# Block-sparse attention and a top-2 expert layer on one core: where keys are scaled, who turns rows, and which banks the products share

## The chip, the cores and the metric

The kernel runs on one core of a Trainium2 chip. The metric is the device time of one execution in microseconds (us). A core has engines with a queue of instructions each: TensorE (PE, matrix products, with its weight loads shown apart as PEld), VectorE (DVE), ScalarE (ACT), GpSimd (POOL) and SyncE (SP), which here only starts DMA transfers. Instructions of one queue run in the order of the code, and semaphores hold an instruction back until what it needs is done. Products land in PSUM, which has eight banks of 128 partitions and 512 numbers of 32 bits.

## The reference, cut to what matters

```python
# q, k, v: 4 batches, 8 heads, 768 positions, 64 numbers a head; blocks of 32 positions
mask = np.abs(blk_i - blk_j) <= 1
mask = mask | (blk_i == 0) | (blk_j == 0) | (blk_i == n_blocks - 1) | (blk_j == n_blocks - 1)
for qb in range(n_blocks):
    for kb in sampled_blocks[qb]:          # 3 sampled blocks for each query block
        mask[qb * block:(qb + 1) * block, kb * block:(kb + 1) * block] = True
scores = np.where(mask, scale * np.matmul(q, k.transpose(0, 1, 3, 2)), -1e9)   # scale = 1/8
attn = exp(scores - max) / sum
x = np.matmul(attn, v) as rows             # 3072 rows of 512 numbers

noisy = x @ w_gate + log1p(exp(x @ w_noise)) * noise      # 8 experts
top2, weights = the two largest of noisy, softmax over the two
out[row] += weight * (relu(x[row] @ w1[e]) @ w2[e])       # for the two experts e of each row
```

## The kernel before, in words

The order of the code is the order on each engine's queue (a manual schedule). Attention comes first, the routing to experts runs between its steps, and the experts follow.

A batch has six tiles of 128 queries (`t`), each in two halves of four heads (`f`); the queries of the first and last block, which see every key, are four further items (`g`, the global rows). `steps` walks over the 64 items of all batches. At step k four items are in work at different stages: `new` (item k+2) gets its scores and its softmax, `now` (item k) has its exponentials turned by PE (`turn`, tile `ptr`), `old` (item k-1) gets its products with v (`av`, into the PSUM tile `po`) and is divided by its sums (`norm`, tile `xr`), and `out` (item k-2) is split into two 16-bit halves by ACT (`high`, L382) and POOL (`low`, L389). Two steps later PE turns the finished rows (`turn_x`, L396) for the routing and the result is copied out to `r_xT` (L397).

PSUM: six banks `ps` for scores and turned exponentials, one bank `po` which `av`, `turn_x` and the routing's products share, and one bank `pog`, in which the global rows' products (`global_av`, L352) gather over a batch.

Keys: `kk` holds a whole batch, loaded by SP in six pieces (`load_k`, L169) while the batch before is in work. For each tile, POOL copies the key blocks that it needs into `kc` (`prefetch_k`, L200 and L201; two buffers), and `scores` (L238) multiplies queries by `kc`, or by `kk` for the global rows (`qg`). The factor 1/8 is put on the queries by POOL (`scale`, L180), once for each tile and each `qg`.

Values: SP loads, for each tile and half of its blocks, the windows of neighbours (L212) and then, block by block, the sampled blocks (L216, each one small transfer whose address is read from a register). POOL writes the columns of weights (`weigh`, L224). `va` and `vb` have three buffers up to the fourth batch and two in it.

Routing: `Router.run` is a generator whose pieces are done at `background`; its products go to `po` as well (L678, L754), and DVE keeps sums in `r_acc` (L756). Its constants, `r_d` (POOL, L543) and `r_tri` (DVE, L545) among them, are made in the first batch. `store` (L586) writes the rows to `x_rows`. Near the end of attention POOL gathers the rows of the experts' first unit (L945), and SP turns them by DMA into `xta` (`xpose`, L955), which the first products of the experts (L1003) read. Weights for them come in pieces and are cut to 16 bits by ACT (`w1s`, L889).

## Time and profile before

| what | us |
|---|---|
| three timed executions | 861.63, 868.29, 869.1 (median 868.29) |
| the profiled execution | 863.63 |
| its span, first to last instruction | 861.8 |
| PE busy in it | 789.2 (92%) |
| DVE, ACT, POOL busy | 568.7, 366.9, 388.1 |

The profiled execution's own time is 1.8 us above its span. The busy times are of the whole span; attention takes the first 318.6 us of it and the experts the rest. Matmuls overlap their weight loads, and the granted clock of PE (PEclk in the rows below) is a share of full speed.

### The profile page before, as it was taken

The numbers are of one execution on the slowest core, as the hardware profiler recorded it, in microseconds if no ns is written. First come the engines' busy times: TensorE is split into PE (matmuls) and PEld (weight loads), VectorE is DVE, ScalarE is ACT, GpSimd is POOL, SyncE is SP. The second block draws the span as 40 slices with busy tenths as digits, with TensorE's granted clock in tenths as the row PEclk, the third lists the DMA queues.
The fourth block names the chain that finished last, engine by engine and source line by source line (L and its number), as shares of the span: only waits on it lengthen the run. The fifth ranks groups of instructions, "written<-read, shape, count | busy, mean of one in ns | idle before, by whom it ended". The sixth has DMA issues, their size and how long they took to land.

```text
span 861.8 us, 25602 instructions
## 1 busy us (share of the span) xinstructions
PE 789.2 (92%) x9823; PEld 484.6 (56%) x9823; DVE 568.7 (66%) x1197; ACT 366.9 (43%) x698; POOL 388.1 (45%) x672
## 2 busy tenths in 40 slices
PE   7878988988876779999999989999999999999995
PEld 4556666666654557566587544554554554554552
DVE  6566888878796537762133378697697796796621
ACT  4747757656653415321022331542642633543500
POOL 5566577667558330132245426426335345323211
PEclk9989999999998889999999999999999999999998
DMA  4686677776688985856169939639538548533301
GB/s 150 179 235 201 185 213 192 209 213 187 193 283 260 250 207 151 196 181 112 49 155 224 242 111 233 191 99 237 173 111 238 164 123 221 164 98 102 100 33 49
DMA packets 119848, 148.92 MB, mean 173 GB/s; under 512 B 69515, under 2 KB 76300, under 8 KB 119714
## 3 DMA queue, kind: packets, MB, share of 16 engines
q1 hardware_dynamic: 107490, 109.22, 48.6%
q0 software_dynamic: 12224, 37.96, 13.6%
q8 instruction: 79, 1.29, 0.6%
q14 instruction: 55, 0.45, 0.2%
HBM read 107.28 MB, written 26.15 MB: 155 GB/s over the span
## 4 chain that ended last, share of the span: by engine, by line
PE 75%; DVE 12%; issue 5%; ACT 3%; POOL 2%; DMA 1%; SPq 0%; POOLq 0%; DVEq 0%; ACTq 0%
PE pc L1089 29%; PE pa L1042 10%; PE ps L238 6%; PE pa L1003 6%; PE pd L1042 5%; PE po L326 4%; PE pd L1003 4%; PE ps L304 3%; DVE m L277 3%; PE pc L1098 3%; PE pc L1042 2%; PE po L396 1%; PE pog L352 1%; DMA va<-in_vx_dram 1%; DVE xr L336 1%
## 5 line engine op out<-in xcount | busy, mean ns | idle before, releaser
L1089 PE MATMUL pc<-w,hh 128*128 128x512 f16 x768 | 228.4, 379 | 0.0
L1122 POOL DMA_INDIRECT out_dram<-y,r_xT x46 | 66.9, 1454 | 210.2 <-DVE y L1121 176.7
L1089 PE MATMUL pc<-w,hl 128*128 128x512 f16 x384 | 145.5, 379 | 0.0
L1089 PEld LDWEIGHTS <-hh 128*128 128x128 f16 x768 | 74.6, 98 | 86.3
L1042 PEld LDWEIGHTS <-w 128*128 128x128 f16 x840 | 82.2, 98 | 63.1
L280 ACT ACTIVATE p<-ps,m 128x256 f32<-128x256 f32 x192 | 75.2, 475 | 62.8 <-DVE m L277 61.2
L1011 ACT ACTIVATE hh<-pa 128x408 f16<-128x408 f32 (+2 forms) x60 | 26.3, 447 | 121.9 <-PE pa L1003 116.4
L200 POOL COPY kc<-kk 128x128 f32 x264 | 69.2, 300 | 14.0 <-PE ps L238 9.1
L277 DVE TENSOR_REDUCE m<-ps 128x2 f32<-128x512 f32 x96 | 61.6, 682 | 17.2 <-PE ps L238 16.9
L893 DVE SCALAR_TENSOR_TENSOR w<-wraw,w 128x1024 f16<-128x1024 f32 (+1 forms) x58 | 65.2, 1127 | 10.6 <-ACT w L889 10.6
L326 PE MATMUL po<-va,ptr 128*32 128x68 f32 x1536 | 57.4, 235 | 14.8 <-DMA va<-in_vx_dram 4.5
L238 PE MATMUL ps<-kc,q 64*32 64x256 f32 x1536 | 58.8, 399 | 7.5 <-POOL q L180 4.5
L1014 DVE SCALAR_TENSOR_TENSOR hl<-pa,hh 128x408 f16<-128x408 f32 (+2 forms) x60 | 30.1, 503 | 51.9 <-ACT hh L1011 51.9
L945 POOL DMA_INDIRECT xg<-x_rows,r_xT x46 | 57.3, 1246 | 14.7 <-issue 14.1
L963 POOL DMA_INDIRECT pv<-out_dram,r_xT x44 | 48.7, 1107 | 32.0 <-issue 29.0
L1089 PEld LDWEIGHTS <-hl 128*128 128x128 f16 x384 | 37.6, 98 | 45.3
L326 PEld LDWEIGHTS po<-va,ptr 128*32 128x32 f32 x1536 | 40.8, 115 | 36.6 <-issue 13.2
L326 PE MATMUL po<-vb,ptr 128*32 128x68 f32 x1536 | 56.6, 232 | 5.2 <-issue 5.2
L889 ACT ACTIVATE w<-wraw 128x1024 f16<-128x1024 f32 (+1 forms) x58 | 56.4, 975 | 6.6 <-DMA wraw<-in_moe_w_dram 6.6
L1121 DVE SCALAR_TENSOR_TENSOR y<-pc,r_xT,pv 128x512 f32<-128x512 f32 x37 | 27.7, 750 | 47.4 <-PE pc L1089 47.4
L304 PE MATMUL ps<-r_ident,p 128*128 128x128 f32 x384 | 54.0, 284 | 0.7 <-issue 0.6
L1003 PEld LDWEIGHTS <-w1s 128*128 128x128 f16 x432 | 43.0, 100 | 13.9 <-issue 0.9
(231 smaller groups left out, 1576.7 us busy)
## 6 DMA issues: line engine op xcount, KB each, us to landing
wraw<-in_moe_w_dram SPq DMA_DIRECT2D x64, 512.0 KB, 4.5
va<-in_vw_dram SPq DMA_DIRECT2D x40, 384.0 KB, 4.8
vb<-in_vx_dram SPq DMA_DIRECT2D x176, 64.0 KB, 3.4
q<-in_qt_dram SPq DMA_DIRECT2D x24, 256.0 KB, 3.3
va<-in_vx_dram SPq DMA_DIRECT2D x88, 64.0 KB, 4.1
kk<-in_kt_dram SPq DMA_DIRECT2D x18, 256.0 KB, 2.9
x_rows<-x SPq DMA_DIRECT2D x16, 256.0 KB, 3.2
out_dram<-x SPq DMA_DIRECT2D x4, 768.0 KB
```

What stands on the lines that cost most here:

```text
L200: nc.gpsimd.tensor_copy(kc[:, j, :, 3 + n], flat[:, bass.ds(self.listed(blk, n), P)].rearrange("p (n c) -> p n c", c=32))
L238: mm = lambda o, l, r: nc.tensor.matmul(o, l, r, start=True, stop=True, skip_group_check=True)
L277: nc.vector.tensor_reduce(m[:, par], s[par].rearrange("p (e c) -> p e c", e=2), axis=AX.X, op=ALU.max, negate=True)
L280: nc.scalar.activation(p[:, 2 * e + par], s[par][:, 256 * e:256 * e + 256], AF.Exp, bias=m[:, par, e:e + 1])
L304: nc.tensor.transpose(t[:, e, c], p[:, 2 * e + par, P * c:P * c + P], self.ident)
L326: nc.tensor.matmul(o[32 * j:32 * j + 32, h], d[:, h % 2, h // 2, x, 32 * j:32 * j + 32], self.values(v[:, self.slot(t, j)], 4 * f + h), st ...
L893: self.nc.vector.scalar_tensor_tensor(lo, t, WS, hi, op0=ALU.mult, op1=ALU.subtract)
L945: nc.gpsimd.indirect_dma_start(out=self.xg[0:m, c + self.place(u)], out_offset=None, in_=self.x_dram[0:nr], in_offset=bass.IndirectOffsetO ...
L1003: nc.tensor.matmul(ph[:, 0:m], w[:, wt, slot, kb % 2 * P:kb % 2 * P + P], r["xt"][:, kb, a, o:o + m], start=i == 0, stop=i == last)
L1042: nc.tensor.matmul(o, w[:, wt, slot, s * P:s * P + P], mv(s, a), start=i == 0 and p in tail, stop=i == 5, skip_group_check=True)
L1089: nc.tensor.matmul(py, h[:, f, o], w(f)[:, x], start=i == 0, stop=i == last)
L1122: d = nc.gpsimd.indirect_dma_start(out=self.out, out_offset=bass.IndirectOffsetOnAxis(ap=r["ix"][0:m, c:c + 1], axis=0), in_=y[0:m], in_of ...
```

## The change

Four things are changed in attention and one call in the experts.

1. `ps_o` gets two banks, used by turns, and `pog` is dropped. `global_av` now puts the products of one tile into a `po` bank, and DVE copies (first tile of a batch) or adds them to the SBUF tile `og`. It is called ahead of the `av` of the same item instead of behind its `norm`.
2. `turn_x` is copied out by ACT instead of DVE.
3. Keys are scaled instead of queries: at the start the two halves of `kk` by DVE and POOL, later each of the six pieces of the next batch by POOL, two steps after its load is issued. The `scale` of `q` and `qg` is gone.
4. The query pool has three buffers instead of four, and queries are loaded at most two tiles ahead.
5. `xpose` of unit 0 (five DMA transposes) is issued by ACT's queue instead of SP's.

```diff
--- before.py
+++ after.py
@@ -72,14 +72,13 @@
         pool = lambda c, name, bufs, **kw: c.enter_context(tc.tile_pool(name=name, bufs=bufs, **kw))
         self.const = pool(ctx, "aconst", 1, side="right")
         self.buf = pool(ctx, "abuf", 1, side="right")
-        self.qp = pool(ctx, "aq", 4, side="right")
+        self.qp = pool(ctx, "aq", 3, side="right")
         self.pp = pool(ctx, "app", 2, side="right")
         self.gp = pool(early, "agp", 3)
         self.sm = pool(ctx, "asm", 4, side="right")
         self.xp = pool(ctx, "axp", 2, side="right")
         self.ps_s = pool(ctx, "ps_s", 6, space=PSUM)
-        self.ps_o = pool(ctx, "ps_o", 1, space=PSUM)
-        self.ps_g = pool(ctx, "ps_g", 1, space=PSUM)
+        self.ps_o = pool(ctx, "ps_o", 2, space=PSUM)
         ep = pool(early, "aeb", 1)
         two = lambda n: ep if n == 2 else self.buf
         J = self.NJ
@@ -90,6 +89,7 @@
         self.qgt = [two(2 - 2 * i).tile([P, self.NP, 64], F32, name=f"qg{i}") for i in range(2)]
         self.ends = [two(2).tile([P, self.HD], F32, name=f"ends{i}") for i in range(2)]
         self.xs = [self.buf.tile([P, self.NP, 2, P], F16, name=f"x{n}") for n in range(2)]
+        self.og = self.const.tile([P, 4, self.W], F32, name="og")
         self.known = self.const.tile([P, self.NB, 2], F32, name="known")
         self.pgt = [self.buf.tile([P, 8, P], F32, name=f"pgt{i}") for i in range(4)]
         self.ident = ident
@@ -176,8 +176,9 @@
     def load_ends(self, b):
         self.nc.sync.dma_start(self.ends[b % 2][64:128], self.vg[b])
 
-    def scale(self, x):
-        self.nc.gpsimd.tensor_scalar(x, x, 0.125, 1.0, op0=ALU.mult, op1=ALU.mult)
+    def scale_k(self, b, i, n, engine):
+        x = self.kk[b % 2][:, i * self.NB // n:(i + 1) * self.NB // n]
+        engine.tensor_scalar(x, x, 0.125, 1.0, op0=ALU.mult, op1=ALU.mult)
 
     def which(self, b, t):
         n = b * self.T + t
@@ -339,19 +340,20 @@
     def global_av(self, b, t):
         nc, W = self.nc, self.W
         va = self.st["v", b, t][0]
-        if t == 0:
-            self.og = self.ps_g.tile([P, 512], F32, name="pog")[:, 0:4 * W].rearrange("p (i r w) -> p i r w", i=2, r=2)
-        for c in range(8):
-            blk = 3 * c + 1
-            if blk // self.NJ != t:
-                continue
+        cs = [c for c in range(8) if (3 * c + 1) // self.NJ == t]
+        o = self.psum()[:, 0:4 * W].rearrange("p (i w) -> p i w", w=W)
+        for c in cs:
             for i in range(2):
                 for r in range(2):
                     for e in range(2):
                         h = 2 * (2 * i + e) + r
-                        nc.tensor.matmul(self.og[64 * e:64 * e + 64, i, r], self.pgt[2 * i + r][0:96, c, 64 * e:64 * e + 64],
-                                         self.values(va[0:96, blk % self.NJ], h), start=c == 0 and i == 0 and r == 0,
-                                         stop=c == 7, skip_group_check=True)
+                        nc.tensor.matmul(o[64 * e:64 * e + 64, 2 * i + r], self.pgt[2 * i + r][0:96, c, 64 * e:64 * e + 64],
+                                         self.values(va[0:96, (3 * c + 1) % self.NJ], h),
+                                         start=c == cs[0] and i == 0 and r == 0, stop=c == cs[-1], skip_group_check=True)
+        if t == 0:
+            nc.vector.tensor_copy(self.og, o)
+        else:
+            nc.vector.tensor_tensor(self.og, self.og, o, op=ALU.add)
 
     def x_tile(self, b, t):
         if ("x", b, t) not in self.st:
@@ -363,7 +365,7 @@
     def global_out(self, b, part):
         nc = self.nc
         if part == 0:
-            self.xgr = self.norm(self.og.rearrange("p i r w -> p (i r) w"), 4)
+            self.xgr = self.norm(self.og, 4)
             self.xg = self.xp.tile([P, 2, 2, P], F16, name="xg", bufs=1)
         elif part == 1:
             nc.scalar.activation(self.xg[:, :, 0], self.xgr.rearrange("p (i r) d -> p i (r d)", i=2), AF.Copy)
@@ -394,7 +396,7 @@
         o = self.psum().bitcast(F16).rearrange("p (c k) -> p c k", c=2 * self.NP)
         for c in range(2 * self.NP):
             nc.tensor.transpose(o[:, c], x[:, c], self.ident16)
-        nc.vector.tensor_copy(xT[:, t].rearrange("p k a c -> p (k a) c"), o)
+        nc.scalar.activation(xT[:, t].rearrange("p k a c -> p (k a) c"), o, AF.Copy)
 
     def warm(self):
         o = self.bank()
@@ -409,13 +411,13 @@
             self.load_k(0, i, 2)
         self.prefetch_q(0, 0)
         self.listed = self.numbers(self.packed, mybir.EngineType.Pool, P)
-        self.scale(self.st["qg", 0])
+        for i, engine in enumerate((self.nc.vector, self.nc.gpsimd)):
+            self.scale_k(0, i, 2, engine)
         for x in self.va:
             self.nc.vector.memset(x[0:96, :, self.HD:], 1.0 / XS)
         for x in self.vb:
             self.nc.vector.memset(x[64:P, :, self.HD:], 1.0 / XS)
         self.prefetch_k(0, 0)
-        self.scale(self.st["q", 0, 0])
         self.load_ends(0)
         self.unlisted = self.numbers(self.masked, mybir.EngineType.SP, 1)
         self.prefetch_v(0, 0, 0)
@@ -427,14 +429,13 @@
         self.prefetch_v(0, 1, 0)
         self.prefetch_v(0, 1, 1)
         self.weigh(0, 1)
-        self.scale(self.st["q", 0, 1])
 
     def steps(self, router, done, background):
         nc, T, B = self.nc, self.T, self.B
         n = len(self.items)
         get = lambda k: self.items[k] if 0 <= k < n else ("none",)
         tg = [(b, t) for b in range(B) for t in range(T)]
-        nq, nz, nk, nv = 3, 2, 2, 2
+        nq, nk, nv = 3, 2, 2
         turns, shares, stores, halves = [], [], [], []
         marks = [(n - 1, self.spread, n // 2, (n % 2 * 2,)) for n in range(4)]
         for k in range(-2, n + 7):
@@ -459,10 +460,10 @@
             self.cut(now)
             background(k, 1)
             if old[0] == "q":
+                if old[3] == 1:
+                    self.global_av(old[1], old[2])
                 self.av(old)
                 self.st[old, "xr"] = self.norm(self.st.pop((old, "o")), 4)
-                if old[3] == 1:
-                    self.global_av(old[1], old[2])
             background(k, 2)
             while shares:
                 b, part = shares.pop(0)
@@ -475,20 +476,17 @@
             if old[0] == "q" and old[3] == 1 and old[2] == T - 1:
                 self.global_out(old[1], 0)
                 shares.append((old[1], 1))
-            if nz < nq and new[0] == "q" and new[3] == 0 and new != ("q", 0, 0, 0):
-                self.scale(self.st[("q",) + tg[nz]])
-                nz += 1
             if new[0] == "q" and new[1] + 1 < B:
                 i = 2 * new[2] + new[3] - 1
                 if i == 2:
                     self.load_g(new[1] + 1)
                     self.load_ends(new[1] + 1)
-                if i == 7:
-                    self.scale(self.st["qg", new[1] + 1])
+                if 2 <= i <= 7:
+                    self.scale_k(new[1] + 1, i - 2, 6, nc.gpsimd)
             if new[0] == "q" and new[3] == 1 and nk < len(tg):
                 self.prefetch_k(*tg[nk])
                 nk += 1
-            if new[0] == "q" and nq < len(tg) and (nq > self.late_) == (new[3] == 1):
+            if new[0] == "q" and nq < min(len(tg), new[1] * T + new[2] + 3) and (nq > self.late_) == (new[3] == 1):
                 self.prefetch_q(*tg[nq])
                 nq += 1
             while halves:
@@ -952,7 +950,7 @@
         if c == 0:
             pool, x = (self.xta, "a") if u % 2 == 0 else (self.xtb, "b")
             r["xt"] = pool.tile([P, self.KB, 2, 7 * P], F16, name="xt" + x)
-        self.nc.sync.dma_start_transpose(out=r["xt"][:, :, :, c * P:(c + 1) * P].rearrange("p k a r -> p (k a) r"),
+        (self.nc.scalar if u == 0 else self.nc.sync).dma_start_transpose(out=r["xt"][:, :, :, c * P:(c + 1) * P].rearrange("p k a r -> p (k a) r"),
                                          in_=self.xg[:, c + self.place(u)])
 
     def gather_prev(self, u):
```

On POOL's queue, in the first batch before the copies of tile 3 (`xe` is the 16-bit form of rows of the tiles that hold global rows, `kk_105` the current batch's keys), there stood before:

```order
L201 COPY kc_107<-kk_105 128x4x96
L389 TENSOR_TENSOR xe<-xr,xe 128x2x128
L180 TENSOR_SCALAR q<-q 128x512
L200 REGISTER_ALU
L200 ISA
L200 COPY kc_108<-kk_105 128x4x32
```

and now (`kk_102` is the current batch's keys, `kk_103` the next batch's):

```order
L202 COPY kc_104<-kk_102 128x4x96
L391 TENSOR_TENSOR xe<-xr,xe 128x2x128
L181 TENSOR_SCALAR kk_103<-kk_103 128x512
L201 REGISTER_ALU
L201 ISA
L201 COPY kc_105<-kk_102 128x4x32
```

The scale there is no longer one of a query tile but one of a piece of the next batch's keys.

Some 40 rows later on the same queue, where the routing's constants are made, there stood before:

```order
L389 TENSOR_TENSOR xe<-xr,xe 128x2x128
L180 TENSOR_SCALAR q<-q 128x512
L224 COPY va_99<-known 128x4x32
L224 COPY vb_102<-known 128x4x32
L543 IOTA r_d 128x128
L549 IOTA r_io_825 128x8
L552 IOTA r_tok 128x6
L554 IOTA r_line 128x128
```

and now:

```order
L391 TENSOR_TENSOR xe<-xr,xe 128x2x128
L181 TENSOR_SCALAR kk_103<-kk_103 128x512
L225 COPY va_96<-known 128x4x32
L225 COPY vb_99<-known 128x4x32
L541 IOTA r_d 128x128
L547 IOTA r_io_821 128x8
L550 IOTA r_tok 128x6
L552 IOTA r_line 128x128
L181 TENSOR_SCALAR kk_103<-kk_103 128x512
```

A second piece of keys stands ahead of the constants in place of a query tile, and a third behind them.

On ACT's queue, at the last weights (`w1s`) before the end of attention, there stood before:

```order
L280 ACTIVATE p<-ps,m 128x256 x4
L889 ACTIVATE w1s<-wraw 128x1024
L306 ACTIVATE ptr<-ps 128x512
L382 ACTIVATE x_113<-xr 128x2x128
L280 ACTIVATE p<-ps,m 128x256 x4
L306 ACTIVATE ptr<-ps 128x512
```

and now:

```order
L281 ACTIVATE p<-ps,m 128x256 x4
L887 ACTIVATE w1s<-wraw 128x1024
L953 DMA_TRANSPOSE xta<-xg 128x8x128 x2
L307 ACTIVATE ptr<-ps 128x512
L384 ACTIVATE x_110<-xr 128x2x128
L399 ACTIVATE r_xT<-po 128x1024
L281 ACTIVATE p<-ps,m 128x256 x4
L953 DMA_TRANSPOSE xta<-xg 128x8x128 x2
L307 ACTIVATE ptr<-ps 128x512
```

The four transposes stand between ACT's own steps, and so does the eviction of the turned x, `r_xT`; a fifth transpose follows two rows later.

## Rows read from the trace of the kernel before

**Rows 1.** Windows: length, busy us per engine (instructions), PEclk, DMA share, GB/s.

```profile
0.00:80.00 80.00, 62.98 (x1381) 43.34 (x1382) 49.94 (x130) 47.80 (x105) 48.59 (x159) 0.96 0.66 188
80.00:235.00 155.00, 134.84 (x3389) 96.64 (x3387) 126.77 (x354) 101.90 (x227) 100.25 (x259) 1.00 0.71 199
235.00:318.60 83.60, 59.72 (x1428) 44.45 (x1428) 55.49 (x162) 32.37 (x79) 47.63 (x102) 0.91 0.90 247
318.60:862.00 543.40, 531.61 (x3628) 300.16 (x3627) 336.50 (x554) 184.80 (x289) 191.59 (x154) 0.99 0.56 151
```

**Rows 2.** PE's waits, 80 to 235 us: total, times, longest.

```profile
PE po L396 <- DVE xr L336: 4.1, 4, 1.4
PE po L678 <- DVE xr L336: 2.4, 2, 1.2
PE po L326 <- DVE r_acc L756: 2.1, 2, 1.5
```

**Rows 3.** Groups by shape, DVE, 0 to 318 us: busy, mean ns.

```profile
L336 DVE TENSOR_TENSOR xr<-po,rc 128x256 f32<-128x256 f32 x48 | 20.4, 425 | 4.0
...
L397 DVE COPY r_xT<-po 128x1024 f16<-128x1024 f16 x24 | 16.4, 683 | 1.7 <-PE po L396 0.9
```

**Rows 4.** Groups by shape, ACT, 0 to 318 us.

```profile
L306 ACT ACTIVATE ptr<-ps 128x512 f32<-128x512 f32 x48 | 28.9, 603 | 27.8 <-PE ps L304 27.5
```

**Rows 5.** Groups by shape, POOL, 0 to 318 us.

```profile
L180 POOL TENSOR_SCALAR q<-q 128x512 f32<-128x512 f32 x24 | 14.8, 619 | 12.1 <-DMA q<-in_qt_dram 12.1
```

**Rows 6.** Line L216 on SP's queue, 80 to 235 us: min/median/max ns.

```profile
L216 SPq DMA_DIRECT2D vb<-in_vx_dram x99: 315/316/1127, 81.3 to 234.9; - x99
```

**Rows 7.** SP's timeline, 133.5 to 140 us: start, duration.

```profile
137.57 0.97 SPq L216 DMA_DIRECT2D vb<-in_vx_dram  x2
```

**Rows 8.** Line L326 on PE, 141 to 143.3 us: first and last start.

```profile
L326 PE MATMUL po<-va,ptr x32: 222/223/247, 142.0 to 142.8; 128*32 128x68 f32 x32
```

**Rows 9.** POOL's timeline, 28 to 56 us: idle before in brackets.

```profile
33.03 0.77 POOL L200 COPY kc<-kk 128x128 f32 x3
...
37.69 0.68 POOL L389 TENSOR_TENSOR xe<-xr,xe 128x256 f16<-128x256 f32 x1
44.69 0.62 POOL L180 TENSOR_SCALAR q<-q 128x512 f32<-128x512 f32 x1 [6.33 <-DMA q<-in_qt_dram]
...
45.73 0.24 POOL L543 IOTA r_d<- 128x128 int32 x1
```

**Rows 10.** DVE's timeline, 37 to 48 us.

```profile
46.01 0.23 DVE L545 TENSOR_SCALAR r_tri<-r_d 128x128 f16<-128x128 int32 x1 [7.96 <-POOL r_d L543]
```

**Rows 11.** PE's timeline, 40 to 57 us.

```profile
47.65 1.96 PE L238 MATMUL ps<-kc,q 64*32 64x256 f32 x30 [1.22 <-DVE ptr L308]
```

**Rows 12.** SP's timeline, 40 to 52 us.

```profile
40.76 1.51 SPq L191 DMA_DIRECT2D q<-in_qt_dram  x1
```

**Rows 13.** Tile kk, 100 to 140 us: issues and landing.

```profile
L169 SPq DMA_DIRECT2D kk<-in_kt_dram x6: 416/526/1302, 109.0 to 132.8; - x6
...
DMA to landing us min/median/max: 2.8/2.8/2.8
```

**Rows 14.** POOL's timeline, 103 to 128 us.

```profile
104.98 0.77 POOL L200 COPY kc<-kk 128x128 f32 x3 [1.57 <-PE ps L238]
```

**Rows 15.** Line L238 on PE, 113 to 127 us: first and last start.

```profile
L238 PE MATMUL ps<-kc,q x96: 372/376/401, 114.6 to 126.2; 64*32 64x256 f32 x96
```

**Rows 16.** Chain of waits, 240 to 320 us: start, us, what.

```profile
291.08 6.83 DMA va<-in_vx_dram
```

**Rows 17.** SP's timeline, 280 to 306 us.

```profile
294.77 0.34 SPq L212 DMA_DIRECT2D va<-in_vw_dram  x1
...
299.69 3.29 SPq L955 DMA_TRANSPOSE xta<-xg  x2
```

**Rows 18.** ACT's timeline, 284 to 319 us.

```profile
289.29 1.07 ACT L889 ACTIVATE w1s<-wraw 128x1024 f16<-128x1024 f32 x1
```

**Rows 19.** Windows, 298 to 302 us.

```profile
298.00:302.00 4.00, 4.00 (x66) 3.56 (x66) 1.43 (x4) 0.00 (x0) 0.00 (x0) 0.50 1.02 167
```

## Prediction, made before the changed kernel ran

> **What bounds the kernel now.** I read the windows first: in the experts' stage, from 318.6 us to the end, TensorE (PE) is busy for 531.6 of 543.4 us, and the diff touches nothing there but who issues five transposes ahead of it. Whatever the change does, it does in the 318.6 us of attention. There PE is idle for 17 us in the first 80, 20 in the next 155 and 24 in the last 84; the reader should see that VectorE (DVE), with 126.8 of 155 us in the middle stretch, is nearly as full as PE [rows 1]. So nothing in the middle stretch can be worth more than some 20 us. Next I read what PE waits for there: the largest items that name the single `po` bank are the turned x behind `xr` (4.1 us), the routing's sums behind `xr` (2.4) and av behind the routing's `r_acc` (2.1) [rows 2].
>
> Then I looked for what stands behind PE, and found SyncE's (SP's) queue. It carries every load of v; L216 alone issues 149 small DMAs in that stretch, 99 of them for `vb`, each 0.32 us at the median [rows 6], with a starting distance of about 0.65 us, since two issued together take 0.97 us of timeline [rows 7]. For tile 10 the last pair of these is issued up to 138.54 (137.57 + 0.97) [rows 7], and PE starts its product with v at 142.0 [rows 8]. With a landing of 2.8 us, which I read from the keys [rows 13], the data are there at 141.3: PE can be 0.7 us earlier in that place, no more, unless SP is too. So I take SP as the pacemaker of the later tiles of each batch; only the first tiles of a batch, beside the global rows, give it a lead.
>
> **Two banks, and the eviction by ScalarE (ACT).** Of PE's waits the three items above make 8.6 us in 155 [rows 2]; the same rate over the 83.6 us after it makes 4.6 more. Not every such wait ends with a second bank, so I take 12 us of these 13.2. DVE loses 24 copies of 0.683 us (16.4 us) and gains 24 adds or copies of 128x272 numbers, which I price as `xr`, 128x256 from the same kind of bank, 0.425 us (10.2 us) [rows 3]: 6.2 us less. ACT gains 24 evictions of 1024 columns. Its 512 columns take 0.603 us [rows 4], so one takes between 0.6 and 1.2; I take 1.0, 24 us in all. ACT is busy 101.9 of 155 us there [rows 1], so this fits beside other work, but the turned x stays in its bank 0.3 us longer than before. Gain if PE alone set the pace: 12 us. Gain that SP's queue lets through: 0.7 us as at tile 10, once in each of four batches and not added up, because SP's issues don't move: about 1 us.
>
> **Keys scaled in place of queries.** GpSimd (POOL) loses 24 scales of 0.619 us [rows 5] and four smaller ones; it gains one half of 128x1536 at the start and 18 scales of 128x512 at the same 0.619. In busy time that is nothing. The start costs at most 3 x 0.619 = 1.9 us on POOL against what it did before, and at 44.69 POOL has 6.33 us of idle time to spend [rows 9], so I charge 0. What matters is the wait. A scale of a piece of the *next* batch's keys waits for that piece's DMA, and behind it on POOL stand the copies `kc` for the current batch, which PE's scores need.
>
> Batch 0: before, the copies of tile 3 run from 33.03 to 37.69, 4.7 us, and only then does POOL wait, for a query load, to 44.69; `r_d` is made at 45.73 [rows 9], DVE's `r_tri` has waited 7.96 us for that [rows 10], and PE's scores start again at 47.65 [rows 11]. After, the first key piece stands ahead of tile 3's copies and takes the place on SP that the query load had, issued at 40.76 [rows 12]. It lands when that one did, at 44.6. Then 0.6 scale, 4.7 copies, 0.7 `xe`, 0.6 next scale, 0.5 the two `known` copies: `r_d` at 51.8, 6.1 us later than 45.73. PE's waits of that place are already behind this chain, so all 6.1 us is on the path.
>
> Batch 1: pieces are issued from 109.0 and land 2.8 us later [rows 13]; with an issue of 1.0 us, the first is there at 112.2 or later (an `x_rows` issue beside it moves this by no more than 0.5). The copies behind it began at 104.98 [rows 14] and now begin at 112.8, 7.8 us later. Before, they ended at 109.7 (4.7 us later) and their scores began at 114.6 [rows 15], 4.9 us of slack: 7.8 - 4.9 = 2.9 us. The scores go through the copies one after the other, so part of this is hidden; I take 2. For the next tile and for the same places of batch 2 I have no row as near and take 2.5 and 0.8, as estimates from this one; batch 3 has no keys to scale. Sum 6.1 + 2 + 2.5 + 0.8 = 11.4 us of delay. Bounds: 0, if the pieces come earlier because SP's queue does, and 11.4.
>
> How much of it is left at the end? SP's issues are not delayed by it as long as the buffers of v are free, and PE, with 12 us fewer waits for the bank, catches up with SP: by the first term it can regain up to 12 us where it is behind. So delay and gain nearly cancel: 11.4 - 12 gives -0.6 where SP sets no pace, and where it does the time can't fall below before's by more than 1. I take +0.5 for the first 235 us.
>
> **Unit 0's transposes on ACT.** SP is relieved of 3.29 us between the two halves of v of the last tile [rows 17]. That is on PE's path only in part: the long wait of this stretch comes earlier, for a `va` that stands in the chain as one transfer of 6.83 us from 291.08 [rows 16]. In the order of after, the first two transposes stand on ACT right behind `w1s`, which ends at 290.36 (289.29 + 1.07) [rows 18], 9.3 us earlier than on SP. The DMA engines are full there: share 0.90 over the whole last stretch [rows 1] and 1.02 in 298 to 302, where PE also runs at a granted clock of 0.50, that is 1.2 GHz, after its wait [rows 19]. So two transposes' transfers get in front of v for tiles 22 and 23. I price that between 0 and 3.3 us, the time the pair takes to issue; nearest is the middle, since other transfers are in flight beside it: +1.7. On the other side SP's next issues come 3.3 us earlier: up to -3.3, of which half reaches PE, -1.6, as the bank and norm chain ends late too. ACT, which issues them, is held for 3.3 us behind `w1s`, at a time when PE waits for `va` anyway; 0. Later q loads for the last tiles put 512 KB into the full stretch: +0.5.
>
> The Trainium skill, "Trainium Kernel Development and Optimization", section Key Constraints, says that DMAs from the SP, ACT and POOL queues all run on the same 16 engines and interleave, and that issuing from several only saves the issuing sequencer's time. By that rule the move is worth at most SP's issue time and the full DMA share agrees with it; taken strictly, the term would be -3.3 and not about 0.
>
> **Sum.** +0.5 (to 235 us), +0.6 (transposes and q), +0.4 for the two more steps on DVE between the last product and the last norm (one add, 0.425 [rows 3]), experts 0: +1.5 us. The profiled execution took 863.6 us, the three timed ones 861.6, 868.3 and 869.1; their mean with the profiled one is 865.7, so the forecast is 867 us. About 1% (8.7 us) is what a measurement of this kernel can tell from no change.
>
> **Rivals.**
> (a) *The bank waits come back.* If SP isn't a hard limit (its issues wait for buffers that PE frees, and come earlier with PE), 12 us return, and the delay on POOL is small because the key pieces come earlier too: 865.7 - 12 = 854. For it: DVE is nearly full in the middle stretch and loses 6 us, and PE's clock is full there [rows 1]. Against it: only 0.7 us of slack at tile 10 [rows 7, 8].
> (b) *POOL stays behind the key pieces* (slower than before). The place is the first scale ahead of `kc` in batches 0 and 1, the price 11.4 us, of which nothing is regained if tiles 4 to 6 and 10 to 12 run at the pace of SP, which then also waits for buffers of v that are freed later; with 1 us back from the banks, 865.7 + 10 = 876. It decides from the point where PE enters the last tile of batch 1 later than SP has its v ready: if the lag there is over 8 us, the batch's slack is used up. For it: `r_tri` waits for POOL already [rows 10]. Against it: PE has idle time to spare in each batch.
> (c) *The change does not do what it says*: the two banks are used by turns, but each next user waits for the same DVE step (`xr` before the turned x, the row sums before the norm), so no wait falls, while the transposes help by SP's 3.3 us: 865.7 - 2 = 864. That falls into the forecast's own range.
>
> **How the numbers follow.** Forecast with (c) together: 0.57, own range 861 to 873 (the terms' bounds: -4 and +6). Rival (a) and cases on its side: 0.21. Rival (b): 0.22. The range that leaves no more than 2 in 10 out reaches to most of (a) and (b): 854 to 876. Faster by over 1% has 0.21, within 1% 0.57, slower by over 1% 0.22.
>
> **What would show it.** In the changed kernel's profile: PE's wait for the bank behind `xr` and `r_acc` nearly gone; POOL idle ahead of a `kk` scale at about 38 to 44 us and at 104 to 112 us, with `kc` behind it; `r_d` at about 52 us; the first scores of batch 1 some 6 us later, of batch 3 within 2 us of before; L397's time on ACT near 1.0 us; the last product with v within 3 us of before. Wrong would make it: key pieces that land before POOL asks for them, SP's issues well ahead of PE in the later tiles, or a first layer of the experts that starts more than 8 us from 318.6 us in either direction.

## The result: a little slower, beyond the interval

| | us |
|---|---|
| before, 20 executions | median 868.44 (861.46 to 874.91) |
| changed, 20 executions | median 874.9 (867.73 to 879.81) |
| ratio, 95% interval | 1.0062 [1.0037, 1.0086] |
| profiled execution of the changed kernel, its span | 878.97, 877.2 |

The forecast said no change that can be measured: 867 us, which is +1.5 us on its base of 865.7 us, the mean of the four executions known then, and 1.4 us below the median of before from 20. The time lies in the range of 854 to 876, but it moved up by 0.62%, some 5.4 us, and the interval excludes no change. The forecast took 1% as the least that a measurement can tell; 20 executions of each kernel told about 0.25%.

The two profiled executions are 15.3 us apart (878.97 and 863.63): the one of before lies near the lower end of its executions and the one of after near the upper end of its own. So the traces show where waits are; how much each is worth is taken from the timed experiments below.

The windows of the changed kernel, cut at its own first product of the experts (332.5 us, against 318.6 before):

```profile
0.00:80.00 80.00, 60.52 (x1279) 40.74 (x1282) 46.71 (x128) 47.17 (x103) 47.85 (x150) 0.91 0.63 183
80.00:235.00 155.00, 136.74 (x3342) 97.71 (x3326) 125.34 (x342) 111.52 (x236) 101.31 (x261) 0.97 0.67 192
235.00:332.50 97.50, 68.63 (x1587) 50.81 (x1588) 57.44 (x175) 44.58 (x96) 46.81 (x100) 0.86 0.83 228
332.50:877.20 544.70, 532.26 (x3628) 300.31 (x3627) 336.32 (x554) 184.80 (x289) 192.88 (x154) 0.99 0.55 151
```

PE's work in the experts takes 532.3 of 544.7 us, against 531.6 of 543.4 [rows 1], so the time was lost in attention. There, PEclk is lower in all three windows (0.91, 0.97 and 0.86, against 0.96, 1.00 and 0.91 [rows 1]); whether that is a cause or follows from PE's waits is not shown. PE's waits for the `po` bank in the middle stretch are now these:

```profile
PE po L398 <- DVE og L356: 3.3, 4, 1.4
PE po L752 <- POOL hot L743: 2.6, 3, 1.4
...
PE po L398 <- DVE xe L377: 1.8, 3, 0.7
PE po L327 <- DVE xr L337: 1.7, 2, 1.4
...
PE po L350 <- DVE xr L337: 1.1, 1, 1.1
```

The three items that the forecast counted, 8.6 us [rows 2], are gone from that list: no turned x waits behind `xr`, no routing sum behind `xr`, no av behind `r_acc`. In place of the first stands a new one, the turned x behind `og`, 3.3 us, and the routing's products now wait 2.6 us for POOL's `hot`. All rows of that list that name `po` add up to 12.3 us, against 16.5 before, so 4.2 us of waits went and not 8.6. From 235 us to the experts the rows that name `po` and no transfer add up to 18.9 us, against 16.4 before: there nothing went. The prices of the steps, DVE's by shape and then ACT's:

```profile
L337 DVE TENSOR_TENSOR xr<-po,rc 128x256 f32<-128x256 f32 x48 | 20.4, 425 | 4.0
...
L356 DVE TENSOR_TENSOR og<-og,po 128x272 f32<-128x272 f32 x20 | 8.6, 430 | 2.4 <-PE po L350 2.3
```

```profile
L399 ACT ACTIVATE r_xT<-po 128x1024 f16<-128x1024 f16 x24 | 24.4, 1021 | 2.3 <-PE po L398 2.3
```

The sum into `og` takes 0.430 us and the eviction of the turned x on ACT 1.021, priced at 0.425 [rows 3] and 1.0. On POOL's timeline in the first batch the wait stands where it was expected:

```profile
45.20 0.62 POOL L181 TENSOR_SCALAR kk<-kk 128x512 f32<-128x512 f32 x1 [13.85 <-DMA kk<-in_kt_dram]
45.76 0.77 POOL L201 COPY kc<-kk 128x128 f32 x3
...
51.05 0.63 POOL L181 TENSOR_SCALAR kk<-kk 128x512 f32<-128x512 f32 x1
...
52.10 0.26 POOL L541 IOTA r_d<- 128x128 int32 x1
```

The first scale of `kk` waited 13.85 us; `r_d` is made at 52.10, against 45.73 [rows 9] and 51.8 in the forecast. On PE's timeline the scores then start again at 54.57, against 47.65 [rows 11], after waits of 7.07 and 6.48 us:

```profile
47.03 1.06 PE L239 MATMUL ps<-kc,q 64*32 64x256 f32 x2 [7.07 <-POOL kc L202]
54.57 1.96 PE L239 MATMUL ps<-kc,q 64*32 64x256 f32 x30 [6.48 <-DVE ptr L309]
```

The same in the second batch, on POOL's timeline, where the forecast had 112.2:

```profile
115.08 0.62 POOL L181 TENSOR_SCALAR kk<-kk 128x512 f32<-128x512 f32 x1 [10.50 <-DMA kk<-in_kt_dram]
```

By tile 10 half of it is regained. SP issues the last loads of that tile's v up to 142.33, PE starts its product at 145.4, 3.1 us later, as against 3.5 us before [rows 7, 8]; PE follows SP there, and both are 3 to 4 us late. SP's timeline and line L327 on PE:

```profile
141.36 0.97 SPq L217 DMA_DIRECT2D vb<-in_vx_dram  x2
```

```profile
L327 PE MATMUL po<-va,ptr x32: 220/223/247, 145.4 to 146.4; 128*32 128x68 f32 x32
```

What the forecast did not have is at the end. SP's waits from 286 to 327 us, its timeline there, and ACT's (rows with ACTq are transfers that ACT issues):

```profile
SPq L217 <- DMA xta<-xg: 6.2, 2, 4.4
...
SPq L217 <- DMA vb<-in_vx_dram: 2.3, 1, 2.3
```

```profile
301.16 0.32 SPq L217 DMA_DIRECT2D va<-in_vx_dram  x1
...
303.12 0.32 SPq L217 DMA_DIRECT2D va<-in_vx_dram  x1
308.17 2.77 SPq L217 DMA_DIRECT2D vb<-in_vx_dram  x2
311.05 0.36 SPq L584 DMA_DIRECT2D x_rows<-x  x1
```

```profile
298.46 1.07 ACT L887 ACTIVATE w1s<-wraw 128x1024 f16<-128x1024 f32 x1
300.18 5.34 ACTq L953 DMA_TRANSPOSE xta<-xg  x2
...
305.94 1.92 ACTq L953 DMA_TRANSPOSE xta<-xg  x1
```

After the load at 303.12 SP stands still until 308.17, 4.4 us of it for the landing of a transpose of the pair that ACT issued from 300.18; the loads of v for tile 22 are issued to the end at 310.94 and PE waits for them:

```profile
PE po L327 <- DMA va<-in_vx_dram: 6.7, 4, 3.1
...
PE po L327 <- DMA vb<-in_vx_dram: 3.2, 2, 2.6
```

That is 9.9 us of waits for v. In the same list of before, from 272 to 320 us, the only such row is

```profile
PE po L326 <- DMA va<-in_vx_dram: 4.5, 2, 2.4
```

and the profiled execution of undo_turn below, without the loss, has 7.7 us, so these lists give a direction and no size. PE's timeline shows which loads of tile 22 it waits for:

```profile
307.82 0.41 PE L327 MATMUL po<-va,ptr 128*32 128x68 f32 x2 [3.15 <-DMA va<-in_vx_dram]
310.44 0.32 PE L327 MATMUL po<-va,ptr 128*32 128x68 f32 x1 [2.21 <-DMA va<-in_vx_dram]
...
313.67 0.29 PE L327 MATMUL po<-vb,ptr 128*32 128x68 f32 x1 [2.60 <-DMA vb<-in_vx_dram]
```

The first two are for loads that SP had issued at 301.16 and 303.12, before it stood still; PE goes on 6.7 and 7.3 us after their issue, with transposes in flight beside them. Before, a `va` took 6.83 us with none in flight [rows 16], so this does not show that the transposes' volume made them longer. Only the third wait, 2.60 us, is for a load behind the stop.

Why a load of v waits for a transpose on another queue is told by the compiled program. Each transfer of SP and of ACT takes one of eight semaphores, DMAHW0 to DMAHW7, by turns in the order of the program, and waits first for the transfer that had the same one before it. These are rows of SP's queue, before and after, at the second half of tile 22's v:

```
before  877 L216 DMA vb_102<-in_vx_dram 32x512 [waits DMAHW2_49]
        878 L212 DMA va_99<-in_vw_dram 96x2x512 [waits DMAHW3_49,PE_49]
        881 L216 DMA va_99<-in_vx_dram 32x512 [waits DMAHW4_49]
after   877 L217 DMA vb_99<-in_vx_dram 32x512 [waits DMAHW2_49]
        878 L213 DMA va_96<-in_vw_dram 96x2x512 [waits DMAHW4_49]
        881 L217 DMA va_96<-in_vx_dram 32x512 [waits DMAHW6_49]
        893 L217 DMA vb_99<-in_vx_dram 32x512 [waits DMAHW3_49,PE_49]
```

Turns 3 and 5 are missing after: transposes on ACT have them, and row 893 waits for the one on DMAHW3.

### The profile page after: what moved, and what is told of

The parts are those of the page before. It is cut to its first block, busy times and chain, and to the rows that moved or that the text cites. A ratio compares the mean times of both kernels' runs of the same rounds, so it can differ in the third digit from the quotient of the medians.

```text
span 877.2 us, 25662 instructions
## 1 busy us (share of the span) xinstructions
PE 798.1 (91%) x9823; PEld 489.6 (56%) x9823; DVE 565.8 (65%) x1198; ACT 388.1 (44%) x722; POOL 388.9 (44%) x663
## 5 line engine op out<-in xcount | busy, mean ns | idle before, releaser
L239 PE MATMUL ps<-kc,q 64*32 64x256 f32 x1536 | 62.6, 406 | 18.1 <-POOL kc L202 8.7
L201 POOL COPY kc<-kk 128x128 f32 x264 | 73.0, 317 | 7.2 <-PE ps L239 7.1
L327 PE MATMUL po<-va,ptr 128*32 128x68 f32 x1536 | 56.2, 234 | 12.5 <-DMA va<-in_vx_dram 6.7
L327 PE MATMUL po<-vb,ptr 128*32 128x68 f32 x1536 | 54.7, 231 | 6.8 <-issue 3.6
L327 PEld LDWEIGHTS po<-va,ptr 128*32 128x32 f32 x1536 | 39.1, 114 | 26.7 <-issue 12.4
L1001 PE MATMUL pd<-xta,w 128*128 128x408 f16 (+1 forms) x144 | 46.8, 333 | 5.2 <-DVE hl L1012 5.1
```

Source lines behind the costliest of these rows:

```text
L201: nc.gpsimd.tensor_copy(kc[:, j, :, 3 + n], flat[:, bass.ds(self.listed(blk, n), P)].rearrange("p (n c) -> p n c", c=32))
L239: mm = lambda o, l, r: nc.tensor.matmul(o, l, r, start=True, stop=True, skip_group_check=True)
L327: nc.tensor.matmul(o[32 * j:32 * j + 32, h], d[:, h % 2, h // 2, x, 32 * j:32 * j + 32], self.values(v[:, self.slot(t, j)], 4 * f + h), st ...
```

## The experiments

All were timed against the kernel before on the same chip; chips differ (before took 868 to 882 us), so only ratios are compared.

**Undo one part, then both.** In the changed kernel, the transposes go back to SP (undo_turn):

```diff
-        (self.nc.scalar if u == 0 else self.nc.sync).dma_start_transpose(
+        self.nc.sync.dma_start_transpose(
```

> The changed kernel with unit 0's five transposes issued by SP again. Theory A (on ACT the transposes stand among the loads of v: a load on SP waited 4.4 and 1.8 us for a transpose's landing, since both take turns in the same eight DMA semaphores): the last stretch gets some 6 us shorter, ratio to the kernel before about 0.999 (867 us), and no load of v waits for a transpose. Theory B (what I priced in the prediction, only shared bandwidth, +1.7 - 1.6 us): no change, ratio 1.005 to 1.006.

Measured: 0.9997 [0.9967, 1.0028]. The loss is gone. SP's waits from 285 to 345 us name no transpose; where a load of v waits there for a transfer, it is one of v:

```profile
SPq L217 <- DMA va<-in_vx_dram: 1.4, 1, 1.4
```

Queries scaled again, and keys not (undo_scale):

```diff
...
+            if nz < nq and new[0] == "q" and new[3] == 0 and new != ("q", 0, 0, 0):
+                self.scale(self.st[("q",) + tg[nz]])
+                nz += 1
...
-                if 2 <= i <= 7:
-                    self.scale_k(new[1] + 1, i - 2, 6, nc.gpsimd)
+                if i == 7:
+                    self.scale(self.st["qg", new[1] + 1])
```

> The changed kernel with the queries scaled on POOL as before, in place of the keys (query pool still three buffers, loads still two tiles ahead). Theory A (POOL's wait for late key pieces delays each batch by 3 to 6 us and is only partly regained): about 5 us shorter, ratio to the kernel before about 1.000, r_d near 46 us. Theory B (the delay is regained behind SP in each batch, as in the forecast): ratio 1.005 to 1.007.

Measured: 1.0052 [1.0015, 1.0088], still slower, as theory B has it; theory A's 1.000 lies outside. But the run takes no wait from POOL. It keeps the query pool of three buffers, with loads at most two tiles ahead, and POOL now waits for loads of q: 51.8 us up to 320 us, where before it waited 12.1. The first row of PE's waits from 80 to 235 us is one that before does not have there:

```profile
PE ps L238 <- POOL q L180: 9.3, 3, 7.8
```

So one wait of POOL was swapped for another; that the forecast's delay is regained rests on scale_only below. Both edits together (banks_only):

> The changed kernel with both undone: queries scaled, transposes on SP; what is left is the two banks, the sums of the global rows in SBUF, the eviction of turned x by ACT, and the query pool of three. Theory A (the loss lies in the two undone parts, the banks help by some 4 us): ratio to the kernel before 0.993 to 0.997 (862 to 866 us). Theory C (adds on DVE and the slower eviction cost, the other parts are harmless): 1.003 or more. If SP's queue lets nothing through, 0.998 to 1.001.

Measured: 1.0016 [0.9982, 1.005]. The gain of theory A is out. A loss as in theory C is not shown, and not excluded by this interval alone, which reaches 1.005; that of undo_turn, with the same banks, reaches 1.0028. In its trace, PE's waits from 80 to 235 us begin with

```profile
PE ps L238 <- POOL q L180: 7.0, 2, 6.6
PE po L397 <- DVE og L355: 5.2, 5, 2.1
PE po L755 <- POOL hot L746: 3.9, 2, 3.5
```

of which the first is again the wait for late queries, 7.0 us, and the second the new one behind `og`, 5.2 us. So this run is not the two banks alone: the query pool of three stays in it.

**One part alone, on the kernel before.** The transposes on ACT and nothing else (turn_only):

> The kernel before with nothing but unit 0's five transposes issued by ACT. Theory A (loads of v wait for transposes): 4 to 7 us longer, ratio 1.005 to 1.008, with waits of SP for a transpose in the last tiles. Theory B (bandwidth only, SP relieved of 3.3 us): 0.998 to 1.002.

Measured: 1.0063 [1.0027, 1.0099], the whole loss from one line. Keys scaled and nothing else (scale_only):

> The kernel before with nothing but the keys scaled in place of the queries (query pool of three, loads two tiles ahead). The forecast's theory (POOL waits for late key pieces, 11.4 us in all, and PE regains most of it): r_d near 52 us, ratio to the kernel before 0.999 to 1.004. Rival (b), not regained because a single bank keeps PE's waits: 1.008 to 1.012.

Measured: 1.0022 [0.999, 1.0055], as the forecast's theory has it; rival (b) is out. The delay is there (`r_d` at 51.6 us), and it is regained with one bank.

**What about the transposes costs?** Three things change when ACT issues them: turns, ACT's time, and when their volume moves. Small transfers at the same places, transposes left on SP (small_dma):

```diff
         at(M0 + 3 + c // 2, ex.xpose, 0, c)
+        at(M0 + 3 + c // 2, ex.spot, c)
...
+    def spot(self, c):
+        self.nc.scalar.dma_start(self.seen[:, 16 * c:16 * c + 16], self.xg[:, c, 0:16])
```

> The kernel before, its transposes on SP as they were, plus five small transfers (16 numbers of each of 128 partitions, read from the gathered rows) issued by ACT exactly where the five transposes stand in the changed kernel; they wait for the same gathers and take the same turns of the eight DMA semaphores, and move next to nothing. Theory A1 (SP's loads of v wait for their turn behind a transfer that itself waits for a gather): at least half of the loss, ratio to the kernel before 1.003 to 1.007. Theory A2 (the loss is the transposes' own length: 3 to 5 us of issue on ACT and up to 6 us in flight): 0.999 to 1.002.

Measured: 1.0041 [1.0005, 1.0077]: five transfers that move next to nothing cost as theory A1 says, though the interval reaches down into theory A2's range; that of small_free below does not. ACT held by arithmetic in the same places (act_hold):

```diff
+    def spot(self, c):
+        for _ in range(4):
+            self.nc.scalar.activation(self.seen, self.seen, AF.Copy)
```

> The kernel before, transposes on SP, plus four ACT copies of 128x256 numbers (some 0.4 us each, 1.7 us) on a scratch tile at each of the five places. It holds ACT for about as long as the transposes' issue does (3.4 us a pair), with no transfer. Theory D (the turned exponentials behind the transposes on ACT come late, and PE's products with them): ratio to the kernel before 1.003 to 1.007. Theories A1 and A2 without that hold: 0.999 to 1.002, since PE waits there for v.

Measured: 1.0007 [0.9973, 1.0041]. ACT's time is not the whole loss; a part of it this interval does not exclude. The hold here is 3.57 us at the first pair, against 6.09 in the changed kernel, where ACT's next step starts at 305.62 and PE waits for v until 310.44. The full transposes on ACT, three steps later (turn_late3):

```diff
-        at(M0 + 3 + c // 2, ex.xpose, 0, c)
+        at(M0 + 6 + c // 2, ex.xpose, 0, c)
```

> The kernel before with unit 0's transposes issued by ACT, but three steps later in the program, behind the last copy of turned exponentials; most of the last loads of v then stand ahead of them in the turns. Theory A (turns): no load of v waits long for a transpose, but the second pair holds ACT ahead of the last rows' eviction, some 2 us: ratio to the kernel before 1.000 to 1.004. Theory B (bandwidth): the same volume still meets the last loads, 1.004 to 1.007.

Measured: 0.9984 [0.9947, 1.0022]. The volume and the queue are the same, the loss is gone. But the volume moves later too: in the trace SP has issued its last load of v before ACT issues the first transpose, so theory B's condition did not come about, and this run does not part the turns from the bandwidth. These are SP's timeline and ACT's:

```profile
312.00 0.97 SPq L216 DMA_DIRECT2D vb<-in_vx_dram  x2
```

```profile
314.84 1.36 ACTq L955 DMA_TRANSPOSE xta<-xg  x1
```

Among SP's waits, a transpose now holds up a store of rows (L586) for 5.2 us, for which the trace names nobody that waits, and no load of v:

```profile
SPq L586 <- DMA xta<-xg: 5.2, 1, 5.2
```

Then the small transfers without a gather to wait for (small_free):

```diff
-        self.nc.scalar.dma_start(self.seen[:, 16 * c:16 * c + 16], self.xg[:, c, 0:16])
+        self.nc.scalar.dma_start(self.seen[:, 16 * c:16 * c + 8], self.seen[:, 16 * c + 8:16 * c + 16])
```

> As the kernel with five small transfers on ACT, at the same places and with the same turns of the eight DMA semaphores, but copying within a scratch tile, so that they wait for no gather. If SP's loads of v lose their time to the gathers that the transfer ahead of them in turn waits for: ratio to the kernel before 0.998 to 1.002. If it is enough that the turn stands on ACT's queue, which reaches that place late: 1.003 to 1.006, as with the wait.

Measured: 1.006 [1.0031, 1.009]. So my refinement, that the gathers make the turn late, is wrong: it is enough that the turn stands on ACT's queue, and no volume is needed. Its trace shows the mechanism alone, in SP's waits, SP's timeline and ACT's:

```profile
SPq L216 <- DMA seen<-seen: 6.8, 3, 4.2
```

```profile
290.96 0.32 SPq L216 DMA_DIRECT2D va<-in_vx_dram  x1
295.77 0.97 SPq L216 DMA_DIRECT2D vb<-in_vx_dram  x2
296.84 0.37 SPq L586 DMA_DIRECT2D x_rows<-x  x1
```

```profile
291.42 0.51 ACTq L961 DMA_DIRECT2D seen<-seen  x1
...
291.97 0.60 ACTq L961 DMA_DIRECT2D seen<-seen  x1
```

ACT comes to the transfers at 291.42 and 291.97, when SP is already among the loads that come after them by turn; SP stops at 291.28 (290.96 + 0.32) and its next load starts at 295.77, 4.2 us of that for a copy of 8 numbers a partition to land. On SP's own queue such waits are shorter; the longest of before from 270 to 320 us is

```profile
SPq L212 <- DMA va<-in_vw_dram: 1.5, 1, 1.5
```

There the transfer eight places back stands eight issues earlier on the same queue; here it has just been issued. PE then waits for the late load, and the chain that ended last runs through a later one of the tiny copies. These are a row of PE's timeline and one of the chain from 240 to 330 us:

```profile
299.73 0.29 PE L326 MATMUL po<-vb,ptr 128*32 128x68 f32 x1 [3.36 <-DMA vb<-in_vx_dram]
```

```profile
297.37 5.21 DMA seen<-seen
```

The same five copies on SP's own queue, which would part the queue from the five added turns, were not run.

**Where the bank's gain went.** Two of three small loads of v are left out from the second batch on, with one bank (half_v) and with two (half_v_banks):

```diff
-            for n, d in enumerate((va[96:128, j], vb[0:32, j], vb[32:64, j])):
+            d3 = (va[96:128, j], vb[0:32, j], vb[32:64, j])
+            for n, d in enumerate(d3 if b == 0 else d3[0:1]):
```

> The kernel before, in which two of the three small loads of sampled value blocks (those into vb) are left out from the second batch on, so that older values are used there. It takes some 44 small issues of 0.65 us, 28 us, from SP in each of three batches. If SP's queue paces attention from the second batch on: 10 to 30 us shorter, ratio 0.965 to 0.988. If PE and DVE pace it: at most 4 us, ratio 0.995 to 1.000, from shorter waits for v at the end alone.

> The kernel with two banks, sums of the global rows in SBUF and eviction by ACT, but queries scaled and transposes on SP, and with the same two of three small loads left out from the second batch on. If SP's queue was what kept the second bank from paying: 6 to 10 us less than the kernel before with those loads left out, a difference of 0.007 to 0.012 in the ratio. If the bank's waits only changed their releaser: within 0.003 of it.

Measured: 0.9928 [0.9891, 0.9965] with one bank, 0.9826 [0.9769, 0.9883] with two. With the loads there, two banks give nothing (1.0016); without them they give 0.0102, some 9 us. So the small loads of v, or what stands behind them on SP's queue, kept the two banks (with `og` and the eviction by ACT, which no run takes apart) from paying. The queries stand behind them: PE's wait for late queries, 7.0 us in banks_only, is not in this stretch of half_v_banks. How much of the 9 us is that wait's stays open, since no run has two banks with the query pool of four. With one bank the time fell by 6.3 us only, less than a pure limit by SP's queue would give and more than none: PE's bank waits stand right behind it. PE's waits from 80 to 235 us, first with one bank and then with two:

```profile
PE po L327 <- DVE xr L337: 4.3, 3, 1.8
PE po L397 <- DVE xr L337: 3.7, 4, 1.6
```

```profile
PE po L398 <- DVE og L356: 2.9, 3, 1.7
...
PE po L327 <- DVE xr L337: 1.3, 2, 0.7
```

Then SP's queue was relieved with all work done: the 24 stores of rows go from SP to POOL, on the kernel before (stores_before) and on the best version below (stores_late_all):

```diff
-        self.nc.sync.dma_start(self.x_dram[r:r + P], x.rearrange("p k a c -> p (k a c)"))
+        self.nc.gpsimd.dma_start(self.x_dram[r:r + P], x.rearrange("p k a c -> p (k a c)"))
```

> The kernel before, with the 24 stores of rows issued by POOL instead of SP. SP loses 24 issues and their waits for POOL's rows (some 4 to 5 us a batch), POOL gains 24 issues of about 1 us. If SP's queue is a limit beside the single bank, as leaving out small loads showed (0.993): ratio 0.993 to 0.999. If POOL's extra time takes it back: 1.000 to 1.005.

> The changed kernel with late transposes on ACT and late scales, and the stores of rows issued by POOL. If SP's queue is what keeps the second bank from paying, the relief is worth more here than with one bank: ratio to the kernel before 0.985 to 0.994. If the sums of global rows on DVE or POOL's time are the limit: 0.995 to 1.001.

Measured: 1.0018 [0.9979, 1.0056] and 0.9971 [0.9941, 1.0001]. The second is not beyond late_all's 0.9974, so this relief is worth nothing that shows. What of a load of v holds PE back, its issue, its turn or its transfer, stays open, since half_v takes away all three.

**A better version.** The changed kernel with late transposes (late_turn_after), and also with the pieces of keys scaled one step later, behind the copies `kc` (late_all):

```diff
-                if 2 <= i <= 7:
-                    self.scale_k(new[1] + 1, i - 2, 6, nc.gpsimd)
...
                 self.prefetch_k(*tg[nk])
                 nk += 1
+            if new[0] == "q" and new[1] + 1 < B:
+                i = 2 * new[2] + new[3] - 1
+                for p in range(6):
+                    if min(p + 3, 7) == i:
+                        self.scale_k(new[1] + 1, p, 6, nc.gpsimd)
```

> The changed kernel with unit 0's transposes still on ACT, three steps later, behind the last loads of v. If the early place among the loads of v is the whole loss, the ratio to the kernel before is 0.997 to 1.001; if scaling or banks carry part of it, 1.002 to 1.005.

> The same, and the pieces of the next batch's keys are scaled one step later and behind the copies of the current batch's keys on POOL. If POOL's wait still costs something after PE's catching up, this is 2 to 5 us faster than the kernel with late transposes alone: ratio to the kernel before 0.993 to 0.998, r_d near 46 us. If SP's queue takes back whatever POOL gives, 0.997 to 1.001.

Measured: 0.9993 [0.996, 1.0026] and 0.9974 [0.9936, 1.0012]. The first undoes the whole loss with the transposes still on ACT. The second puts POOL's wait behind the copies: its longest wait for keys falls from 14.2 us in the first to 6.4, and `r_d` is made at 44.3. The step between the two, 0.0019, is not clear of noise.

```profile
L544 POOL IOTA r_d<- x1: 247/247/247, 44.3 to 44.3; 128x128 int32 x1
```

The second version is faster than the changed kernel (1.0062), and not shown to be faster than the kernel before.

## Why the prediction was wrong, step by step

- **The step that failed** is the sum of "Unit 0's transposes on ACT": +1.7 for bandwidth, -1.6 because "SP's next issues come 3.3 us earlier", +0.5 for queries. I treated the two queues as joined by bandwidth alone. Measured, the move costs 0.63% by itself (turn_only) and 0.65% as the difference of after and undo_turn, some 5.5 us, with the other sign for SP: its next loads come later, because they wait for turns that ACT holds. Bandwidth is not needed for it: five tiny copies on ACT cost 0.41% and 0.60% with the transposes left on SP. Whether the transposes' volume adds to it in the changed kernel, or SP's relief takes some off, is not shown. ACT's time, which I put at 0, was 6.09 us and not 3.3, but PE waited for v beyond it. A sign of being wrong that the prediction named came: the experts' first layer starts 13.9 us behind 318.6. It is a weak one, since the two profiled executions are 15.3 us apart and the timed change is 5.4 us.
- The rule of the Trainium skill ("Trainium Kernel Development and Optimization", Key Constraints) that issuing from several engines only saves the sequencer's issue time would have made this term -3.3. Here the second queue cost 5.5 us instead (turn_only), and the rule has no cost for it.
- **Keys scaled** went as written: `r_d` within 0.3 us of the forecast, the wait in the second batch 10.5 us, PE late by 6.9 us in the first batch and by 3.4 us at tile 10, and in the timed runs 1.0022 alone. In the changed kernel it has no price from a run, since undo_scale has a wait for queries in its place. That the delay is regained was right, and rival (b) with its 11.4 us was not; but the forecast let PE regain it by "12 us fewer waits for the bank", and scale_only regains it with one bank.
- **Two banks.** The forecast's 12 us of waits that end became 4.2 us in the middle stretch and none behind it: the three items went, and new ones behind `og` and `hot` came. Rival (c) had that, with other steps. The sum did not suffer from it, because it let through only "about 1 us" for SP's sake, and banks_only agrees with that size. It does not show the reason, since its wait for queries is a rival to SP's loads of v; that SP's issue time is the limit was only argued, and the stores speak against it. half_v and half_v_banks show that rival (a), at 12 us, would have been near with fewer loads of v: 9 us. The slack of 0.7 us at tile 10 was worked out with the landing of keys, 2.8 us; L216's own loads land 3.5 us behind their issue at the median, which leaves none.
- **Experts**: forecast 0; 544.7 against 543.4 us in the two traces.

Without the transposes' own +0.1 the terms were +1.4 us, and undo_turn measured -0.3 us (0.9997), not to be told from it. So the forecast fell by one term; that the others agree in their sum does not show that each is right.

## What to carry to other kernels

A transfer that is moved to another engine's queue may still be tied to the old one: look in the compiled program for which semaphore's turn each transfer takes, and keep a turn on a late queue from standing ahead of loads that PE waits for. Placing the same transfers behind the last of those loads cost nothing, where five tiny copies ahead of them cost as much as the real ones. A second buffer may pay only if what feeds its users can run ahead: take away some of the feed for one run before counting the waits as gain. And when one part of a change is undone, look in the trace for what the rest does without it, as the query pool of three did here.

## What was not expected of the hardware

A copy of 8 numbers a partition held SP for 4.2 us (small_free), for its landing, and another stands in the chain with 5.21 us. A pair of transposes took 5.34 us to issue on ACT's queue at 300.18, in a stretch where the pair took 3.29 us on SP's [rows 17].
